# Fewer, wider loads of ready weight blocks, a summing transfer for one token group, and a late conversion with two load buffers

## The chip, the cores and the metric

The kernel runs on one core of a Trainium2 chip. The time is device microseconds of one execution, the median of several runs. The core's engines run side by side and each takes its instructions in order: TensorE (PE) multiplies, VectorE (DVE) and ScalarE (ACT) work element by element, GpSimd (POOL) does little arithmetic and issues transfers that add, and SyncE (SP) issues nearly all other transfers.

## The reference

Three layers follow one another: a masked attention over 2304 tokens with 8 heads of 64, a mixture of 8 experts whose weights per token come from eight normalizations by rows and columns, and a gated layer behind a row norm. All of it is wanted in float32.

```python
def _moe_ref(x, w_gate, w1, w2):
    ...
    for e in range(E):                       # E = 8, w1[e] 512 x 1024, w2[e] 1024 x 512
        h = np.maximum(x @ w1[e], 0.0)
        ye = h @ w2[e]
        out += P[:, e:e + 1] * ye
    return out

def _moe2_ref(x, w_gate, w_val, w_out, rms_g):   # w_gate, w_val 512 x 1536, w_out 1536 x 512
    rms = np.sqrt(np.mean(x * x, axis=-1, keepdims=True) + 1e-06)
    xn = x / rms * rms_g
    g = xn @ w_gate
    silu = g * (1.0 / (1.0 + np.exp(-g)))
    val = xn @ w_val
    return silu * val @ w_out
```

The last layer's three matrices, in_moe_w_gate, in_moe_w_val and in_moe_w_out in the profile, arrive as float64 and are turned into float32 on the chip.

## The kernel before, in words

**Split numbers.** A float32 product is made on PE from two rounded parts of each operand, a high one (made by ACT) and a low one (by DVE), with three matmuls. The 2304 tokens are three groups of 768 (qd 0, 1, 2), each of six tiles of 128 tokens.

**Fast products.** A block product of two by two blocks is done with seven products of sums of blocks instead of eight. The sums of x lie in DRAM, xdt for the experts and xnd for the last layer, and are loaded with 768-KB transfers (L1147). The sums of weights, "ready blocks", stand in w1t, for the last layer also in last_r, in slots of xt, and in w2t. Each of PE's products at L1215 is six matmuls of 128x384; the results go from PSUM through copies on ACT (L1383, L1401) and sums on DVE (L1247, L1404, L1418) in slots of a buffer fa: there are eight of these slots (zs), of 384 columns. The finished hidden values are split again (L1240, L1243) into ht and hx.

**The experts.** Expert 0 runs beside the attention, until about 480 us. Seven experts, two halves of the hidden width and three token groups make 42 groups of work, each of 14 products at L1215 and 14 units of nine matmuls at L1817. Units leave their sums in PSUM, and evict_1 takes them out to acc: an ACT copy (L1838) or a DVE addition (L1849), after which ACT multiplies by the token's weight (L1874) and POOL adds the piece by a transfer to y1d in DRAM (L1881). Only in the last expert's second half does DVE multiply and add straight from PSUM (L1843, 21 instructions for a token group); its first half has loaded y1d into acc by an adding transfer (L1883).

**The norm.** When a token group is complete, its rows are squared (ACT L1448), scaled (L1458), transposed by PE (L1465) and multiplied by rms_g (DVE L1466). norm_blocks then makes the seven sums and splits them (ACT L1482, DVE L1483, L1498 to L1504), and SP stores them in xnd (L1492 for the first three, L1516 for the others). For each tile the parts are built in the same few buffers (spare), so a tile's split waits until the store of the tile before has left them. This goes on during the next token group's units, and for the last group during the last layer's first products.

**The last layer.** Nine passes, three thirds of the hidden width by three token groups; each has 28 products at L1215 and 24 matmul groups into the output (L729 to L731), which DVE adds to acc (L2112) or ACT copies (L2110). The ready blocks of the first third are made during the experts by first_combos and kept in w1d in DRAM. ready_combos (L938) loads them: eight transfers earlier, and the other 32 in one row, behind the experts' last units.

**The conversion.** convert makes one half block of 128x256 numbers: load of the float64 halves to cv (L828, L831), seven DVE instructions (L836 to L860), store to m2g, m2v or m2o (L864). There are 72 of these items. 40 run in the expert stage and 32 from the second pass of the last layer on, in one load buffer; the stored tile t is also one buffer. m2o is loaded again (L1080) for w2t, where ACT (L1083) and DVE (L1086) split it.

**What sets the order.** A Background object counts slots, one for each product or unit. Queues of steps hang on it (fin, prep, prep2, conv); each step has a lag in slots behind the step before it. Everything is written in one order at build time, engines and the SP queue keep to it, and a wait holds up all that is behind on the same engine. At most eight transfers of SP are under way at once.

Of the kernel before, what the change touches and what calls it, by code (L numbers as in the profile page):

```python
# [8 lines left out]
F32 = mybir.dt.float32  # L9
F32R = mybir.dt.float32r  # L10
U32 = mybir.dt.uint32
# [103 lines left out]
def kernel(  # L115
# [48 lines left out]
    CONV_WAIT = (6, 4)  # L164
    PRE_WAIT = 6
    PRE_UNITS = 12
    LAG = 12
    TURN_AT = (29, 30, 31, 32, 33, 34), (32, 33, 34, 35, 36, 37)
# [650 lines left out]
    def convert(nm, f, half):  # L819

        n = KC * P // 2
        raw = cv[:, : 2 * n].bitcast(U32)
# [45 lines left out]
    def conversion(items, wait, quick=False):  # L868

        for n, (nm, f, half) in enumerate(items):  # L870
# [4 lines left out]
            step = 1 if quick else STEP  # L875
            conv.add([(wait, head), (step, number), (step, tail)], tag)
            if n + 1 < len(items):
                conv.add([(step, whole), (0 if quick else 1, convert(*items[n + 1])[0])], tag)
                conv.add([(0 if quick else 2, store)], tag)
            else:  # L880
                conv.add([(step, whole), (WRITE, store)], tag)


    SPOTS = (0, 1, 5, 2, 3, 4, 6)

    def first_combos(s, c):
# [35 lines left out]
        def store(src, n0, n):  # L922
            for i, t in enumerate((h[:, : src.shape[1]], src)):
                nc.sync.dma_start(out=w1d[:, s, i, n0 : n0 + n, c], in_=t.rearrange("p (k n) -> p k n", k=n))
# [3 lines left out]
            (1, lambda: store(raw, 0, 4)), (5, lambda: high(both)), (STEP, lambda: low(both)),  # L928
            (1, lambda: store(both, 4, 3)),
        ]  # L930

    def ready_combos(g, j, part):

        at = region(g, j)
        for k, n in ((), ((0, 2),), ((3, 2),), ((5, 1), (6, 1)), ((2, 1),))[part]:
            p = SPOTS.index(k)
            for i in range(2):
                nc.sync.dma_start(  # L938
                    out=at(7 * i + k, n).bitcast(F32).rearrange("p (k m) -> p k m", k=n),
                    in_=w1d[:, j, i, p : p + n].rearrange("p k c m -> p k (c m)"),  # L940
                )
# [111 lines left out]
    def prepare_1(g, j, part=None):  # L1053
# [5 lines left out]
        if g == E:  # L1059
            prep.add([(PACE, lambda: ready_combos(g, j, part))], ("w1", g, j))  # L1060
# [159 lines left out]

    def h_slot(i):
        t = ht_flat[:, 768 * i : 768 * (i + 1)] if i < 4 else hx[:, i - 4]
        return t[:, :TH], t[:, TH:]
# [301 lines left out]
    with tc.manual_schedule():  # L1525
# [300 lines left out]
        def evict_1(n, k):  # L1826
# [36 lines left out]
            if (g, hh) == (E - 1, 1) and k >= 5:  # L1863
                scales[k - 5].add(norm_scale(qd, 3 * (k - 5)), ("scale", qd))
# [364 lines left out]
```

## Time and profile before

| | us |
|---|---|
| median of 3 runs | 2128.11 (2127.64 to 2130.58) |
| profiled execution | 2127.49, of which its span 2124.7 |
| PE busy | 2027.7, 95% of the span |
| DVE busy | 1594.4, 75% |
| ACT busy | 1312.5, 62% |
| POOL busy | 268.4, 13% |
| mean granted clock of PE | 0.985 of full speed |

A profile is of one execution. Attention with expert 0 fills the time to about 480 us, the other experts that to about 1632, the last layer the rest. The changeover from experts to last layer lies between 1570 and 1735 us. An idle stretch of an engine is given in square brackets with what ended it; where several things were waited for, the one that came last by the profile is named.

### The profile page before, as it was taken

To read this page: it belongs to the slowest core of one execution; us is meant where nothing else is said; L and a number is where in the kernel's file an instruction comes from. 1 tells how busy PE (TensorE), PEld (TensorE's weight loads), DVE (VectorE), ACT (ScalarE), POOL (GpSimd) and SP (SyncE) were. 2 spreads that over 40 slices of the span, in tenths; PEclk is the share of its full clock that TensorE was granted. 3 is DMA by queue.
4 is the path that set the end of the run, shared out by engine and by line. 5 is a ranking of instruction groups with operands and counts; after the bars stand their busy time and mean duration, and the time that the engine had idled before them with its cause. 6 is when DMAs were issued, how large, how long until landed. Compare 5 with 4: busy or idle time off the path is not lost. (4 is left out here: it accounts for less than half of the span.)

```text
span 2124.7 us, 37479 instructions
## 1 busy us (share of the span) xinstructions
PE 2027.7 (95%) x13611; PEld 1926.7 (91%) x13611; DVE 1594.4 (75%) x3387; ACT 1312.5 (62%) x2932; POOL 268.4 (13%) x304
## 2 busy tenths in 40 slices
PE   8999998999999999999999999999997689999998
PEld 7888888999999999999999999999997578888897
DVE  4677656878787887868778787887987567877644
ACT  6766334777776877778777777777755333423422
POOL 6444200001111111111111111111100000000000
PEclk9999999999999999999999999999998899999999
DMA  7687675577978979798887978869657764443331
GB/s 188 165 247 197 197 250 181 210 247 178 279 210 216 264 204 296 202 245 224 237 250 193 264 185 239 225 165 281 185 158 261 232 202 155 131 174 115 129 134 60
DMA packets 358249, 434.24 MB, mean 204 GB/s; under 512 B 80944, under 2 KB 260336, under 8 KB 358064
## 3 DMA queue, kind: packets, MB, share of 16 engines
q1 hardware_dynamic: 319296, 363.48, 52.2%
q0 software_dynamic: 38768, 68.36, 18.6%
q8 instruction: 107, 1.75, 0.3%
q14 instruction: 78, 0.64, 0.1%
HBM read 301.75 MB, written 130.02 MB: 203 GB/s over the span
## 5 line engine op out<-in xcount | busy, mean ns | idle before, releaser
L1215 PE MATMUL ub<-xt,w1t 128*128 128x384 f32 x2328 | 475.4, 341 | 29.2 <-DVE fa L1404 14.2
L1215 PEld LDWEIGHTS ub<-xt,w1t 128*128 128x128 f32 x2328 | 401.5, 192 | 36.5 <-DVE fa L1404 14.8
L1215 PE MATMUL ub<-xx,w1t 128*128 128x384 f32 x1956 | 396.4, 339 | 10.5 <-DVE fa L1247 3.8
L1817 PE MATMUL db<-w2t,ht 128*128 128x256 f32 x2772 | 383.0, 283 | 6.5 <-DVE acc L1849 3.3
L1817 PEld LDWEIGHTS db<-w2t,ht 128*128 128x128 f32 x2772 | 368.2, 190 | 11.1 <-DVE acc L1849 7.1
L1817 PE MATMUL db<-w2t,hx 128*128 128x256 f32 x2520 | 349.6, 284 | 7.2 <-DVE acc L1849 3.8
L1215 PEld LDWEIGHTS ub<-xx,w1t 128*128 128x128 f32 x1956 | 333.8, 190 | 18.4 <-DVE fa L1247 6.9
L1817 PEld LDWEIGHTS db<-w2t,hx 128*128 128x128 f32 x2520 | 333.2, 190 | 16.2 <-DVE acc L1849 12.5
L1247 DVE TENSOR_TENSOR fa<-ub,fa 128x384 f32<-128x384 f32 x360 | 199.2, 554 | 149.2 <-PE ub L1215 134.9
L1366 ACT ACTIVATE fa<-fa 128x384 f32<-128x384 f32 x252 | 132.3, 525 | 180.6 <-DVE fa L1247 180.3
L1881 POOL DMA_DIRECT2D y1d<-acc x99 | 113.9, 1150 | 843.6 <-ACT acc L1874 378.3
L1243 DVE TENSOR_TENSOR ht<-fa,ht 128x384 fp32r<-128x384 f32 x344 | 189.4, 552 | 33.0 <-ACT ht L1240 32.3
L1240 ACT ACTIVATE ht<-fa 128x384 fp32r<-128x384 f32 x344 | 177.4, 518 | 37.9 <-DVE fa L1418 37.4
L1874 ACT ACTIVATE acc<-acc,prob 128x256 f32<-128x256 f32 (+1 forms) x351 | 190.8, 573 | 14.3 <-DVE acc L1849 14.0
L1243 DVE TENSOR_TENSOR hx<-fa,hx 128x384 fp32r<-128x384 f32 x316 | 174.4, 552 | 27.9 <-ACT hx L1240 26.6
L1240 ACT ACTIVATE hx<-fa 128x384 fp32r<-128x384 f32 x316 | 162.1, 519 | 48.7 <-DVE fa L1418 47.4
L1321 DVE TENSOR_TENSOR fa<-fa 128x384 f32<-128x384 f32 x336 | 185.6, 552 | 5.3 <-ACT fa L1362 0.3
L1358 ACT COPY fa<-ub 128x384 f32<-128x384 f32 x252 | 119.7, 475 | 94.9 <-PE ub L1215 90.8
L1849 DVE TENSOR_TENSOR acc<-db,acc 128x768 f32<-128x768 f32 (+1 forms) x117 | 143.0, 1222 | 33.3 <-PE db L1817 32.1
L1838 ACT COPY acc<-db 128x768 f32<-128x768 f32 x156 | 124.5, 798 | 19.8 <-PE db L1817 16.8
L1383 ACT COPY fa<-ub 128x384 f32<-128x384 f32 x108 | 51.4, 477 | 92.0 <-PE ub L1215 91.8
L981 DVE TENSOR_TENSOR w1t<-fa,w1t 128x256 fp32r<-128x256 f32 (+1 forms) x160 | 83.4, 525 | 11.1 <-ACT w1t L978 10.7
(261 smaller groups left out, 3070.2 us busy)
## 6 DMA issues: line engine op xcount, KB each, us to landing
xt<-xdt SPq DMA_DIRECT2D x111, 768.0 KB
xx<-xdt SPq DMA_DIRECT2D x92, 768.0 KB
y1d<-acc POOLq DMA_DIRECT2D x72, 384.0 KB, 7.0
y1d<-acc POOLq DMA_DIRECT2D x36, 768.0 KB, 8.1
xt<-xnd SPq DMA_DIRECT2D x25, 768.0 KB
xx<-xnd SPq DMA_DIRECT2D x24, 768.0 KB
fa<-in_moe_w_dram SPq DMA_DIRECT2D x56, 256.0 KB
raw<-in_moe_w_dram SPq DMA_DIRECT2D x52, 256.0 KB
```

Source lines behind the costliest of these rows:

```text
L1215: nc.tensor.matmul(ps[:, :TH], w[i][:, c], x[:, k, c], start=first and c == 0 and n == 0, stop=c == 1 and n == 2, skip_group_check=True,)
L1240: nc.scalar.activation(h[0], src, func)
L1243: engine.tensor_tensor(out=h[1], in0=src, in1=h[0].bitcast(F32), op=ALU.subtract)
L1247: nc.vector.tensor_tensor(out=out, in0=ps, in1=more, op=ALU.add)
L1321: nc.vector.tensor_tensor(**kw)
L1358: nc.scalar.copy(z[nm], ps)
L1366: nc.scalar.activation(z[nm], z[nm], AF.Relu)
L1817: nc.tensor.matmul(spot(k, m), hm[x], w[y], start=BEGIN[k] and r == 0 and m in FIRST[PAIR[k]] and i == 0, stop=r == 1 and i == 2, skip_gro ...
L1838: nc.scalar.copy(a, ps)
L1849: nc.vector.tensor_tensor(out=a, in0=ps, in1=a, op=ALU.add)
L1874: nc.scalar.activation(a, a, AF.Copy, scale=prob[:, tile_of(qd, b), g : g + 1])
L1881: nc.gpsimd.dma_start(out=y, in_=t, accum_op=ALU.add)
```

## The change

The edits, in the order of the diff:

- The ready blocks lie in w1d in the order in which they are used, so that they come back with 14 transfers instead of 40; each of the eight stores of first_combos becomes ten transfers instead of four. The last two column blocks come back as they lie, in pieces of up to 128x3072 (L2094 of the new file).
- The late conversion (late_conversion) uses a second load buffer, which is two neighbouring slots of the eight in fa, from the second pass to the end. A load is issued two items ahead. The conversion rests in every third pass. Eight items of w_out more are done in the expert stage, 48 instead of 40, with a pause of 4 slots instead of 6 before each; the late ones have 3.5 instead of 4.
- Of the last expert, the middle token group (qd 1) goes the way of the other experts: its first half adds to y1d, its second half is copied or added to acc, weighted by ACT, and y1d is added to acc by three transfers of POOL. Its norm starts 14 and 16 slots later (GATHER), and its tiles are transposed three slots later, the sixth of them in the last layer's first pass.

New line numbers are higher by 10 to 21 in the places below: L938 is L949 and L2094, L1080 L1090, L1083 L1093, L1147 L1157, L1448 L1466, L1458 L1476, L1482 L1500, L1492 L1510, L1516 L1534, L1240 L1258, L828 and L831 L829 and L832, L864 L865.

```diff
     EARLY_AT = (5, 6)
     SUMS = 24
-    CONV_WAIT = (6, 4)
-    PRE_WAIT = 6
+    CONV_WAIT = (4, 3.5)
+    PRE_WAIT = 4
+    GATHER = 14, 16
     PRE_UNITS = 12
     LAG = 12
-    TURN_AT = (29, 30, 31, 32, 33, 34), (32, 33, 34, 35, 36, 37)
+    TURN_AT = (29, 30, 31, 32, 33, 34), (35, 36, 37, 38, 39)
     BLOCK_LAG = (1.0, 1.0, 0.85)
...
-    def convert(nm, f, half):
+    def convert(nm, f, half, raw=None):
 
         n = KC * P // 2
-        raw = cv[:, : 2 * n].bitcast(U32)
+        raw = (cv[:, : 2 * n] if raw is None else raw).bitcast(U32)
...
-    def conversion(items, wait, quick=False):
+    def late_conversion(items, wait, other):
+
+        made = [convert(*x, (None, other)[n % 2]) for n, x in enumerate(items)]
+        conv.add([(WRITE, made[0][0]), (0, made[1][0])], items[0][:2])
+        for n, (_, head, number, tail, whole, store) in enumerate(made):
+            tag = items[n][:2]
+            conv.add([(wait, head), (1, number), (1, tail), (1, whole)], tag)
+            if n + 2 < len(made):
+                conv.add([(0, made[n + 2][0])], tag)
+            conv.add([(0, store)], tag)
...
-        def store(src, n0, n):
-            for i, t in enumerate((h[:, : src.shape[1]], src)):
-                nc.sync.dma_start(out=w1d[:, s, i, n0 : n0 + n, c], in_=t.rearrange("p (k n) -> p k n", k=n))
+        def store(src, spots):
+            for i, t in enumerate((h, src)):
+                for at, k, n in spots:
+                    nc.sync.dma_start(
+                        out=w1d[:, s, i, k : k + n, c],
+                        in_=t[:, P * at : P * (at + n)].rearrange("p (k n) -> p k n", k=n),
+                    )
 
         return load, [
             (PRE_WAIT, sums_1), (STEP, sums_2), (STEP, lambda: high(raw)), (STEP, lambda: low(raw)),
-            (1, lambda: store(raw, 0, 4)), (5, lambda: high(both)), (STEP, lambda: low(both)),
-            (1, lambda: store(both, 4, 3)),
+            (1, lambda: store(raw, ((0, 0, 2), (2, 5, 1), (3, 2, 1)))), (5, lambda: high(both)), (STEP, lambda: low(both)),
+            (1, lambda: store(both, ((0, 3, 2), (2, 6, 1)))),
...
-    def ready_combos(g, j, part):
-
-        at = region(g, j)
-        for k, n in ((), ((0, 2),), ((3, 2),), ((5, 1), (6, 1)), ((2, 1),))[part]:
-            p = SPOTS.index(k)
-            for i in range(2):
-                nc.sync.dma_start(
-                    out=at(7 * i + k, n).bitcast(F32).rearrange("p (k m) -> p k m", k=n),
-                    in_=w1d[:, j, i, p : p + n].rearrange("p k c m -> p k (c m)"),
-                )
+    def ready_combos(j, part):
+
+        k, n = ((0, 0), (0, 2), (3, 2), (5, 2), (2, 1))[part]
+        if n:
+            to = w1_flat[:, 3584 * j : 3584 * (j + 1)].rearrange("p (i k m) -> p i k m", i=2, k=7)
+            nc.sync.dma_start(
+                out=to[:, :, k : k + n].bitcast(F32), in_=w1d[:, j, :, k : k + n].rearrange("p i k c m -> p i k (c m)")
+            )
...
+        def pair(self):
+            n = next(n for n in range(7) if all(any(x is y for x in self.free) for y in z_all[n : n + 2]))
+            self.free = [x for x in self.free if not any(x is y for y in z_all[n : n + 2])]
+            return fa[:, 1536 + TH * n : 1536 + TH * n + 512]
...
+    zs = Store(z_all)
...
+            direct = (g, hh) == (E - 1, 1) and qd != 1
+            if not direct and k in (0, 2, 3, 4):
                 bg.drain(("expert", qd, half, col if half else None))
                 nc.scalar.copy(a, ps)
-            elif (g, hh) == (E - 1, 1):
+            elif direct:
...
+                if not direct:
+                    scales[k - 5].follow([(GATHER[k - 5], lambda: None)], ("scale", qd))
                 scales[k - 5].add(norm_scale(qd, 3 * (k - 5)), ("scale", qd))
...
-                elif g < E - 1:
+                elif g < E - 1 or (hh, qd) == (0, 1):
...
-        conv_items += [(nm, f, half) for f in range(NG, 2 * NG) for nm in "gv" for half in range(2)]
-        conv_items += [("o", f, half) for f in range(NG, 2 * NG) for half in range(2)]
+        conv_items += [(nm, f, half) for f in range(NG, 2 * NG) for nm in "gvo" for half in range(2)]
...
-                conversion(conv_items[24:40], CONV_WAIT[0])
+                conversion(conv_items[24:48], CONV_WAIT[0])
...
-        for j in (2, 3):
-            for part in range(1, 5):
-                ready_combos(E, j, part)
+        for j, parts in (
+            (2, ((last_r[:, :1792], 0), (x_slot(gone_x)[:, :1280], 7), (last_r[:, 1792:], 12), (x_slot(gone_x)[:, 1280:], 13))),
+            (3, ((w2t[:, 0:3].rearrange("p f s n -> p (f s n)"), 0), (xt_flat[:, 7680:8192], 12))),
+        ):
+            ready = w1d[:, j].rearrange("p i k c m -> p (i k c m)")
+            for t, at in parts:
+                nc.sync.dma_start(out=t.bitcast(F32), in_=ready[:, 256 * at : 256 * at + t.shape[1]])
...
+            conv.paused = n % NQD == NQD - 1
             if n == 1:
                 conv.yields = False
-                conversion(conv_items[40:], CONV_WAIT[1], True)
+                late_conversion(conv_items[48:], CONV_WAIT[1], zs.pair())
...
+                            if step == 0:
+                                turn_tile(1, 5, db[5], spares[NGP - 2])
```

**Order of instructions, place 1.** SP, between the x loads of the first pass and the norm stores of the last group (w1t, last_r, xt, w2t hold ready blocks; xnd<-acc and xnd<-cv are those stores). Before, from the m2o loads on:

```order
L1080 DMA fa<-m2o 128x512
L1492 DMA xnd<-acc 128x6x128 x2
L1080 DMA fa<-m2o 128x512
L938 DMA w1t<-w1d 128x256 x6
L938 DMA w1t<-w1d 128x512 x4
L938 DMA w1t<-w1d 128x256 x6
L938 DMA last_r<-w1d 128x512
...
L938 DMA xt<-w1d 128x256
L938 DMA w2t<-w1d 128x256 x2
L1516 DMA xnd<-acc 128x4x128 x2
L1516 DMA xnd<-acc 128x2x128
```

Now:

```order
L1090 DMA fa<-m2o 128x512 x2
L949 DMA w1t<-w1d 128x2x256
L949 DMA w1t<-w1d 128x2x512 x3
L949 DMA w1t<-w1d 128x2x256
L2094 DMA last_r<-w1d 128x1792
L2094 DMA xt<-w1d 128x1280
L2094 DMA last_r<-w1d 128x256
L2094 DMA xt<-w1d 128x256
L2094 DMA w2t<-w1d 128x3072
L2094 DMA xt<-w1d 128x512
L1510 DMA xnd<-acc 128x6x128 x2
L1534 DMA xnd<-acc 128x4x128 x2
```

Eleven wide loads stand where 32 stood. The pair of L1492 stores, which stood between the two m2o loads, now comes behind the loads.

**Place 2.** ACT, at the end of the experts (w2t<-fa is the split of a loaded m2o, acc<-acc,cv the scaling of a tile's rows, cv<-acc the squares). Before:

```order
L1458 ACTIVATE acc<-acc,cv 128x512 x2
L1240 ACTIVATE ht<-fa 128x384
L1458 ACTIVATE acc<-acc,cv 128x512
L1240 ACTIVATE hx<-fa 128x384 x2
L1240 ACTIVATE ht<-fa 128x384
L1482 ACTIVATE acc<-acc 128x512
L1482 ACTIVATE acc<-acc 128x256
L1083 ACTIVATE w2t<-fa 128x512
L1448 ACTIVATE cv<-acc 128x512
L1482 ACTIVATE acc<-acc 128x256
```

Now:

```order
L1476 ACTIVATE acc<-acc,cv 128x512
L1466 ACTIVATE xt,cv<-acc 128x512
L1476 ACTIVATE acc<-acc,cv 128x512
L1093 ACTIVATE w2t<-fa 128x512
L1466 ACTIVATE cv<-acc 128x512
L1476 ACTIVATE acc<-acc,cv 128x512
L1466 ACTIVATE cv<-acc 128x512
L1476 ACTIVATE acc<-acc,cv 128x512 x2
L1466 ACTIVATE cv<-acc 128x512
L1500 ACTIVATE acc<-acc 128x512
L1500 ACTIVATE acc<-acc 128x256
```

The scalings of a group's last tiles stood ahead of the m2o split; now three of them stand behind it.

**Place 3.** SP, in the second pass of the last layer (cv and fa<-in_moe_w are loads of conversion items, m2o, m2g, m2v<-cv their stores, xx and xt<-xnd the x loads of the next pass). Before:

```order
L828 DMA cv<-in_moe_w_out_dram 128x512
L864 DMA m2o<-cv 128x256
L1147 DMA xx<-xnd 128x2x768 x2
L1147 DMA xt<-xnd 128x2x768
L828 DMA cv<-in_moe_w_out_dram 128x512
L864 DMA m2o<-cv 128x256
L1147 DMA xt<-xnd 128x2x768 x3
L828 DMA cv<-in_moe_w_out_dram 128x512
```

Now:

```order
L832 DMA fa<-in_moe_w_val_dram 128x2x256
L865 DMA m2g<-cv 128x256
L832 DMA cv<-in_moe_w_val_dram 128x2x256
L865 DMA m2v<-cv 128x256
L1157 DMA xx<-xnd 128x2x768
L832 DMA fa<-in_moe_w_val_dram 128x2x256
L865 DMA m2v<-cv 128x256
L1157 DMA xx<-xnd 128x2x768
L1157 DMA xt<-xnd 128x2x768 x2
L832 DMA cv<-in_moe_w_gate_dram 128x2x256
```

Loads alternate between cv and fa, and each stands ahead of the store of an item; the stores still come from cv alone.

## Rows read from the trace of the kernel before

**Rows 1.** The page's part 1: engine, busy us (share of the span), instructions.

```profile
PE 2027.7 (95%) x13611; PEld 1926.7 (91%) x13611; DVE 1594.4 (75%) x3387; ACT 1312.5 (62%) x2932; POOL 268.4 (13%) x304
```

**Rows 2.** 480 to 1560: width, PE, PEld, DVE, ACT, POOL, clock, DMA share, GB/s.

```profile
480.00:1560.00 1080.00, 1069.76 (x7503) 1056.23 (x7502) 882.90 (x1766) 813.18 (x1694) 136.75 (x123) 1.00 0.84 226
```

**Rows 3.** Waits of PE, whole span: us in total, times, longest us.

```profile
PE ub L1215 <- DVE fa L1404: 18.2, 6, 14.0
```

**Rows 4.** Timeline of PE: start us, us, instruction, count [idle before <-releaser].

```profile
1602.07 2.29 PE L1817 MATMUL db<-w2t,hx 128*128 128x256 f32 x9 [3.34 <-DVE acc L1843]
...
1660.66 2.29 PE L1215 MATMUL ub<-xt,w1t 128*128 128x384 f32 x6 [13.96 <-DVE fa L1404]
1662.75 1.05 PE L1465 MATMUL db<-ident,acc 128*128 128x128 f32 x4
```

**Rows 5.** Timeline of ACT, changeover.

```profile
1632.29 0.63 ACT L1083 ACTIVATE w2t<-fa 128x512 fp32r<-128x512 f32 x1 [6.06 <-PE ub L1215]
...
1658.80 0.42 ACT L1482 ACTIVATE acc<-acc 128x256 fp32r<-128x256 f32 x1 [12.85 <-DMA xnd<-acc]
```

**Rows 6.** Timeline of SP, changeover: DMA issues.

```profile
1614.86 0.87 SPq L1147 DMA_DIRECT2D xt<-xnd  x2
...
1634.06 8.24 SPq L938 DMA_DIRECT2D w1t<-w1d  x16
...
1654.90 1.73 SPq L1516 DMA_DIRECT2D xnd<-acc  x3
```

**Rows 7.** Last layer in pieces, one pass long (columns as in rows 2).

```profile
1731.49:1782.40 50.91, 48.11 (x240) 43.89 (x240) 35.59 (x90) 17.53 (x36) 0.00 (x0) 0.97 0.52 178
1782.40:1830.73 48.33, 47.26 (x240) 42.53 (x240) 43.70 (x111) 22.71 (x49) 0.00 (x0) 1.00 0.30 94
1830.73:1886.52 55.79, 48.83 (x241) 42.10 (x241) 44.35 (x110) 18.61 (x39) 0.00 (x0) 1.00 0.53 182
1886.52:1939.20 52.68, 48.84 (x240) 44.00 (x241) 41.49 (x100) 15.52 (x33) 0.00 (x0) 0.97 0.46 162
1939.20:1987.25 48.05, 46.23 (x241) 42.71 (x241) 31.44 (x62) 18.59 (x40) 0.00 (x0) 1.00 0.16 52
...
2034.69:2082.11 47.42, 46.21 (x240) 42.68 (x240) 23.13 (x42) 13.78 (x28) 0.00 (x0) 1.00 0.41 150
```

**Rows 8.** Waits of DVE, 1700 to 2125.

```profile
DVE cv L836 <- DMA cv<-in_moe_w_out_dram: 11.9, 9, 2.7
...
DVE cv L836 <- DMA cv<-in_moe_w_val_dram: 5.9, 3, 3.7
...
DVE cv L837 <- DMA m2o<-cv: 1.1, 5, 0.3
```

**Rows 9.** Lines of DVE, 1570 to 1612: shapes, count | busy us, mean ns.

```profile
L1843 DVE SCALAR_TENSOR_TENSOR acc<-db,prob,acc 128x256 f32<-128x256 f32 x18 | 7.6, 477 | 1.5 <-PE db L1817 1.5
...
L1843 DVE SCALAR_TENSOR_TENSOR acc<-db,prob,acc 128x512 f32<-128x512 f32 x3 | 2.1, 743 | 0.0
```

**Rows 10.** Lines of DVE, 480 to 1560.

```profile
L1849 DVE TENSOR_TENSOR acc<-db,acc 128x768 f32<-128x768 f32 x70 | 66.8, 955 | 0.7
```

**Rows 11.** 10-us pieces of the changeover (columns as in rows 2).

```profile
1620.00:1630.00 10.00, 9.55 (x76) 9.22 (x75) 8.67 (x18) 0.42 (x1) 0.00 (x0) 0.94 1.03 404
...
1650.00:1660.00 10.00, 0.00 (x0) 0.00 (x0) 0.76 (x2) 1.20 (x4) 0.00 (x0) 0.60 0.95 302
```

**Rows 12.** Timeline of SP: that item's load, and the store before it.

```profile
1862.26 0.37 SPq L831 DMA_DIRECT2D cv<-in_moe_w_val_dram  x1
...
1863.52 0.33 SPq L864 DMA_DIRECT2D m2v<-cv  x1
```

**Rows 13.** Timeline of DVE: one item's first and second instruction.

```profile
1869.59 0.29 DVE L836 TENSOR_SCALAR cv<-cv 128x256 uint32<-128x256 uint32 x1 [3.70 <-DMA cv<-in_moe_w_val_dram]
...
1870.04 0.29 DVE L837 TENSOR_SCALAR cv<-cv 128x256 f32<-128x256 f32 x1 [0.15 <-DMA m2v<-cv]
```

**Rows 14.** Lines of DVE, 1731 to 1987: one of an item's seven instructions.

```profile
L854 DVE SCALAR_TENSOR_TENSOR cv<-cv 128x256 f32<-128x256 uint32 x30 | 12.8, 426 | 1.0
```

More of the change, by code (lines that the diff above doesn't have):

```diff
@@ L866, in convert, with conversion @@
         return load, head, number, tail, whole, store
-    def conversion(items, wait, quick=False):
+    def late_conversion(items, wait, other):
[7 more added lines that the diff above has]
+            conv.add([(0, store)], tag)
+    def conversion(items, wait):
         for n, (nm, f, half) in enumerate(items):
@@ L874, in conversion @@
                 conv.add([(WRITE, load)], tag)
-            step = 1 if quick else STEP
-            conv.add([(wait, head), (step, number), (step, tail)], tag)
+            conv.add([(wait, head), (STEP, number), (STEP, tail)], tag)
             if n + 1 < len(items):
-                conv.add([(step, whole), (0 if quick else 1, convert(*items[n + 1])[0])], tag)
-                conv.add([(0 if quick else 2, store)], tag)
-            else:
-                conv.add([(step, whole), (WRITE, store)], tag)
-    SPOTS = (0, 1, 5, 2, 3, 4, 6)
+                conv.add([(STEP, whole), (1, convert(*items[n + 1])[0]), (2, store)], tag)
+            else:
+                conv.add([(STEP, whole), (WRITE, store)], tag)
     def first_combos(s, c):
@@ L1059, in prepare_1 @@
         if g == E:
-            prep.add([(PACE, lambda: ready_combos(g, j, part))], ("w1", g, j))
+            prep.add([(PACE, lambda: ready_combos(j, part))], ("w1", g, j))
         else:
@@ L1219, in product, with h_all @@
         bg.matmuls(6, TH)
+    def h_all(i):
+        return ht_flat[:, 768 * i : 768 * (i + 1)] if i < 4 else hx[:, i - 4]
     def h_slot(i):
-        t = ht_flat[:, 768 * i : 768 * (i + 1)] if i < 4 else hx[:, i - 4]
-        return t[:, :TH], t[:, TH:]
+        return h_all(i)[:, :TH], h_all(i)[:, TH:]
     class Store:
@@ L1234, in give @@
             self.free.append(x)
-    zs = Store(fa[:, 1536 + TH * n : 1536 + TH * (n + 1)] for n in range(8))
+        def pair(self):
+            n = next(n for n in range(7) if all(any(x is y for x in self.free) for y in z_all[n : n + 2]))
+            self.free = [x for x in self.free if not any(x is y for y in z_all[n : n + 2])]
+            return fa[:, 1536 + TH * n : 1536 + TH * n + 512]
+    z_all = [fa[:, 1536 + TH * n : 1536 + TH * (n + 1)] for n in range(8)]
+    zs = Store(z_all)
     hslots = Store(range(8))
@@ L1835, in evict_1 @@
                 a = a[:, :, 256 * col : 256 * (col + 1)]
-            if (hh == 0 or g < E - 1) and k in (0, 2, 3, 4):
+            direct = (g, hh) == (E - 1, 1) and qd != 1
+            if not direct and k in (0, 2, 3, 4):
                 bg.drain(("expert", qd, half, col if half else None))
                 nc.scalar.copy(a, ps)
-            elif (g, hh) == (E - 1, 1):
+            elif direct:
                 if k in (0, 2, 3):
@@ L1856, in evict_1 @@
                     prepare_2(E, (0, 2, 1, 3)[k - 3])
-            if (hh == 0 or g < E - 1) and k in (1, 5, 6):
+            if not direct and k in (1, 5, 6):
                 args = (g, hh, qd) + ((1, 0) if k == 1 else (0, None) if k == 5 else (1, 1))
```

## The prediction, made before the changed kernel ran

> **What bounds the kernel now.** I read the page's first part, then PE's waits of the stretch between the experts and the last layer, then the timelines of the engines named there, then equal pieces of the last layer. TensorE (PE) is busy 95% of the span [rows 1], so only the places where it stands still, or runs at the lower of its two clock levels, are to be had. In the expert stage there is next to nothing: from 480 to 1560 us it stands still for 10.2 of 1080 us while VectorE (DVE) is 82% busy [rows 2]. Two places remain.
>
> The first is the changeover. PE waits 18.2 us in six places for one line of VectorE, 14.0 of it at a single product [rows 3]; the row transposes behind that product start only at 1662.75 [rows 4]. The reader should go back along the chain: PE waits for DVE, DVE for ScalarE (ACT), and ACT waits 12.85 us, from 1645.95 to 1658.80, for the store xnd<-acc, whose source it is to overwrite [rows 5]. SP issues that store only at 1654.90, after 32 loads of ready blocks that began at 1634.06 [rows 6]. These follow a load of m2o that stood behind seven 768-KB loads of x from 1614.86 on, and the ACT conversion that needs it starts at 1632.29 [rows 5, 6]. So it is one transfer queue, not arithmetic.
>
> The second is the late conversion. Seven pieces of the last layer, each a pass long, run from one late eviction to the next. The ones without conversion take 47.42 us; the four with most of it take 50.91, 48.33, 55.79 and 52.68 [rows 7]: 18.0 us too many, with 0.6 in the fifth, 18.7 in all. VectorE waits there for loads of raw halves 11.9 and 5.9 us [rows 8].
>
> **Part by part: A, the changeover.** Call the time when the m2o load lands T; it was 1632.3. Three things move.
>
> (1) The middle token group's evictions. Before, 21 VectorE instructions, 7.6 + 2.1 = 9.7 us [rows 9]. After, four go to ACT as copies, and three stay on VectorE as one instruction each, two of 0.955 us [rows 10] and one of twice the width, about 1.8 (an estimate by width): 3.7 us. VectorE is relieved by 6 us between 1577 and 1605, and PE's 3.34 us wait at 1602.07 for such an eviction [rows 4] goes. The stores of x that release the seven loads depend on that stretch, so the loads can start earlier: 2 us if only part of the relief arrives, 5 if also the lower clock after it goes (the nine matmuls there take 2.29 us). I take 3.5. The 17.4 us from 1614.86 to 1632.3 are bytes (5.5 MB at about 0.33 MB/us) and stay. T is then about 1629.
>
> (2) The ACT conversion of m2o now stands ahead of the last three row scalings (second pair of order listings), so PE's transposes wait for T as well. This costs PE nothing of its own: what stands behind has until the stores land. But it leaves PE idle before T and makes it do two units and eight products after T.
>
> (3) The ready loads. 5.77 MB in 11 loads instead of 6.29 MB in 32, and the first two xnd stores (0.39 MB each) of the last group now stand behind all of them (first pair of listings), as the wide store of 1654.90 did before. Each load waits only for free blocks, so they begin about T+2. What does the queue move? 302 GB/s in 1650 to 1660 with its engines 95% busy, on pieces of 1 and 2 KB; 404 GB/s in 1620 to 1630 on the x loads' 3-KB pieces [rows 11]. Of the new loads 3.67 MB come in whole rows of up to 12 KB, so I price them at 404 (9.1 us), the other 2.1 MB and the second m2o load at 302 (7.8 us), and the two stores at 302 (2.6 us): the stores land at T+21.5. Then an ACT copy, three VectorE steps and a transpose follow, 2.5 us: PE goes on at T+24 = 1653, where it stood at 1662.75 before [rows 4]. A = -10 us. Bounds: everything at 302 GB/s and T only 2 us earlier gives 1630.3 + 2 + 22.6 + 2.5 = 1657.4, so -5; all at 404 and T 5 earlier gives 1627.3 + 2 + 16.9 + 2.5 = 1648.7, so -14.
>
> The Trainium skill, DMA: Bandwidth & Descriptors, section "Anatomy of one DMA", fits a transfer as 2.0 us plus bytes at 436 GB/s. By an estimate from that page the 5.77 MB would take 15.2 us, and A would be about -12; no row here shows 436 GB/s, the best is 404.
>
> **B, the rest of the changeover.** The same transposes, splits and stores follow as before, shifted; their waits stay. They now meet the x loads of the next pass a little sooner: between 0 and +3, taken +1.
>
> **C, the late conversion.** Eight of 32 items leave, and pass 2 (of nine, from 0) and pass 5 rest. From the order of instructions, items begin in passes 1 to 5 as 7, 7, 8, 7, 3 before and 8, 0, 8, 8, 0 after. The items that leave are those of the two cheap passes: 48.33 - 47.42 = 0.9 us [rows 7], and 0.6. The dear passes, 1, 3 and 4, are those with x loads; two of them get one item more. At 3.49/7 and 5.26/7 us each that is +1.2. Net -0.3.
>
> The second load buffer is the question. Before, SP issues the next load and right behind it the store of the item just made, at 1862.26 and 1863.52 [rows 12]. The next item's first instruction waits 3.70 us for the load; its second, which overwrites the stored tile, waits a further 0.15 for the store [rows 13]. So the store lands within half a microsecond of the load. Over the last layer the second instruction waits only 1.1 us for m2o stores [rows 8], because the first has already waited. The tile that is stored has no second buffer after the change, and the third pair of listings shows the store still behind a load. Prefetching takes away the wait that is named and leaves the one beneath it. I take 0.3 us of gain for each of some ten waits, against heads that come half a slot sooner and wait that much longer: 0 together. C = 0, with +4 if the heads' half slot is paid in full, and -9 if half of the 18.7 us goes.
>
> **D, two of eight product slots.** The second buffer takes two of the eight slots that hold a product on its way from PSUM, through all later passes. In the order of instructions 30 instead of 15 of 108 ACT copies then wait for a VectorE reader, 19 of them one that is only two to four instructions back. The nearest price is what PE lost at that reader before, outside the changeover: 18.2 - 14.0 = 4.2 us in five places [rows 3]. Twice as many such waits may cost as much again; with PE's lead as it is they may cost nothing. Between 0 and +4, taken +1.5.
>
> **E, the expert stage.** Eight items of seven VectorE instructions (289 to 426 ns, the longest in [rows 14]; together 2.43 us) are 19.5 us more, on an engine with 197 us to spare [rows 2]. They run with pauses of 4 slots instead of 6, and end at the same product as before. Nothing, or half as much again as PE's 10.2 us of standing still there, 5 us; taken +1. The 48 more stores on SP, 64 KB each or less, ride in the time before the next x loads: 0.
>
> **Sum.** -10 + 1 + 0 + 1.5 + 1 = -6.5, against the profiled execution's 2127.5: 2121.0. The median of the runs is 0.6 us above that execution: **2121.5 us**.
>
> **The rivals.** R1, prefetch pays: the store needs no longer than the work between two items, and only the load's wait was real. Half of the excess goes, C = -9, 2112.5 us. For it: the load is the wait that is named, 17.8 us of it. Against: the store's 0.15 us right behind. The Trainium skill, DMA: Bandwidth & Descriptors, section "Rules for kernel authors", advises issuing a transfer early and waiting late; followed here, it gives this rival's time, and the row on the store speaks against it.
>
> R2, the changeover only moves: the loads go on at 302 GB/s, T comes 2 us sooner, later waits return 2 more. A + B = -5 + 3, with D and E 2128.0. For it: the stores still stand behind nearly as many bytes.
>
> R3, slower: six slots are too few. Its place is the ACT copy of each product in passes 1 to 8. If a pass loses 2 us there (16 rounds at 1 us), D is +16: 2136. It decides from about 1.5 us a pass. The piece from 1782.40 on, with VectorE 90% busy (43.70 of 48.33 us), lost only 0.9 [rows 7], which speaks against it; for it speaks that slots were never this few.
>
> R4, the whole block runs at 404 GB/s and PE keeps its higher clock: A = -14, B = 0, 2116.5 us.
>
> **Chances.** Forecast 0.43, R1 0.20, R2 0.20, R3 0.10, R4 0.07. A measurement of this kernel tells about 0.2%, 4.3 us, from no change: faster means below 2123.9. R1, R4 and four fifths of the forecast lie there, 0.62; R2 and the rest of the forecast are the same, 0.28; R3 is slower, 0.10. The range leaves out R3 and the lower end of R1: 2110 to 2131.
>
> **What would show it.** Changeover: m2o landing near 1629, one PE gap before it and one ending at 1650 to 1657 whose chain leads to xnd<-acc, and no 32-fold block on SP. Conversion: VectorE's waits at the first instruction of an item nearly gone, and waits for m2 stores at the second of about the same sum; pieces with conversion still 3 to 8 us over 47.4. If those waits vanish too, C was wrong and R1 holds. Slots: pieces without conversion at 47.4 to 47.9; above 48.5 R3 is at work. Experts: PE idle from 480 to 1560 us below 15 us. The forecast fails if T does not come earlier, or if the store is not what ends last.

## The result and the profile after

The changed kernel takes 2156.5 us (median of 4 runs, 2153.5 to 2159.9) where the kernel before takes 2128.8: ratio 1.013, 95% interval 1.011 to 1.015. It is 28 us slower, where 2121.5 with 2110 to 2131 was forecast. The profiled execution took 2156.46 us, its span 2154.7.

PE's work is the same, 2029.9 us instead of 2027.7 [rows 1]; PE waits more. To find where, I compared the times of one and the same instruction in both traces. The evictions' ACT copies (L1838, now L1857) are good marks, since they come in the same order in both. The 141st of them, shortly before the expert stage ends:

```profile
1416.88 0.80 ACT L1838 COPY acc<-db 128x768 f32<-128x768 f32 x1
```

in the kernel before, and in the changed one

```profile
1445.19 0.80 ACT L1857 COPY acc<-db 128x768 f32<-128x768 f32 x1 [0.18 <-PE db L1835]
```

So 28.3 us were lost by then. The 21st copy stands at 508.19 and 506.44; the **expert piece** between the two marks takes 908.7 us before and 938.8 after. From the 141st copy to the first late eviction (1731.49 and 1759.74), the **changeover piece**, it is 314.6 and 314.6; from there to the last late eviction (2082.11 and 2111.26), the **last-layer piece**, 350.6 and 351.5. All of the loss lies in the expert stage, the stage that was priced at +1. The row that answers to [rows 2] shows it: in the same 1080 us, PE stands still for 33.9 us instead of 10.2 and gets 228 fewer matmuls done, while DVE is busy less, not more.

```profile
480.00:1560.00 1080.00, 1046.08 (x7275) 1029.12 (x7275) 867.94 (x1766) 794.55 (x1654) 134.59 (x121) 0.99 0.83 222
```

DVE's waits for transfers in the expert stage, 480 to 1560 (us in total, times, longest), add up to 69.8 us:

```profile
DVE cv L909 <- DMA cv<-m2v: 16.3, 2, 8.6
...
DVE cv L838 <- DMA m2g<-cv: 16.1, 6, 4.1
...
DVE cv L838 <- DMA m2o<-cv: 11.8, 4, 4.1
...
DVE cv L837 <- DMA cv<-in_moe_w_val_dram: 9.4, 2, 5.0
DVE cv L837 <- DMA cv<-in_moe_w_out_dram: 8.5, 2, 5.2
...
DVE cv L838 <- DMA m2v<-cv: 3.4, 2, 1.9
DVE cv L837 <- DMA cv<-in_moe_w_gate_dram: 3.2, 1, 3.2
...
DVE cv L909 <- DMA cv<-m2g: 1.1, 1, 1.1
```

In the kernel before they were 21.6 us:

```profile
DVE cv L837 <- DMA m2g<-cv: 7.2, 3, 3.2
...
DVE cv L901 <- DMA cv<-m2g: 4.9, 1, 4.9
DVE cv L901 <- DMA cv<-m2v: 2.8, 1, 2.8
...
DVE cv L836 <- DMA cv<-in_moe_w_val_dram: 2.5, 1, 2.5
DVE cv L836 <- DMA cv<-in_moe_w_out_dram: 1.9, 1, 1.9
...
DVE cv L837 <- DMA m2v<-cv: 1.1, 2, 0.7
DVE cv L836 <- DMA cv<-in_moe_w_gate_dram: 0.9, 1, 0.9
...
DVE cv L837 <- DMA m2o<-cv: 0.3, 1, 0.3
```

L909 is the first instruction of a block sum (first_combos), L837 and L838 the first two of an item. The largest stall shows how it comes about. SP, in the changed kernel:

```profile
936.49 1.14 SPq L1157 DMA_DIRECT2D xt<-xdt  x2
937.68 1.29 SPq L903 DMA_DIRECT2D cv<-m2v  x2
```

Then DVE, and behind it PE:

```profile
943.01 0.42 DVE L994 TENSOR_TENSOR fa<-fa 128x256 f32<-128x256 f32 x1
952.02 0.62 DVE L909 TENSOR_TENSOR cv<-cv 128x128 f32<-128x128 f32 x2 [8.59 <-DMA cv<-m2v]
```

```profile
954.10 2.29 PE L1225 MATMUL ub<-xx,w1t 128*128 128x384 f32 x6 [6.52 <-DVE fa L1265]
```

The two loads of the block sum, 128 KB each, were issued at 937.7 behind two 768-KB loads of x, and their reader could start 14 us later. DVE came to that reader after 5.8 us, stood there for 8.59, and all that PE waited for stood behind it; PE then ran its next six matmuls at the lower clock (granted 0.50 from 952 to 954), 2.29 us instead of the 1.21 of the six before the stall. Over these 14 us (columns as in [rows 2]) the transfer engines were full:

```profile
938.00:952.00 14.00, 9.58 (x69) 9.38 (x68) 3.41 (x7) 5.06 (x11) 1.86 (x2) 0.91 1.06 274
```

The pause of 6 slots had been the cover for such a load, and the change cut it to 4. The Trainium skill, DMA: Bandwidth & Descriptors, section "Queues, rings and completion order", says that each DMA engine takes the descriptors of a queue's ring in their order; these rows agree as far as they go, 14 us for 256 KB issued behind x loads on the same queue. But order is not all of it: 14 us at 274 GB/s are some 3.8 MB, more than the 1.5 MB just ahead. Three more x loads had been issued since 929.9, and two adding transfers of POOL, on another queue, took 11.1 and 10.4 us in the same stretch. How much each of them cost, no run separates.

Only a quarter of the 69.8 us (17.4) is at block sums. At items, 21.1 us are for loads and 31.3, the most, at L838 for the store of the item before, which frees the one tile t: the pause covered both.

In the changeover (timeline of ACT, then of SP and of PE):

```profile
1661.70 0.63 ACT L1093 ACTIVATE w2t<-fa 128x512 fp32r<-128x512 f32 x1 [13.99 <-DMA fa<-m2o]
...
1684.35 0.94 ACT L1500 ACTIVATE acc<-acc 128x512 fp32r<-128x512 f32 x2 [3.77 <-DMA xnd<-acc]
```

```profile
1644.85 0.87 SPq L1157 DMA_DIRECT2D xt<-xnd  x2
...
1663.46 2.48 SPq L949 DMA_DIRECT2D w1t<-w1d  x5
```

```profile
1663.61 1.12 PE L1483 MATMUL db<-ident,acc 128*128 128x128 f32 x4 [13.42 <-ACT acc L1476]
...
1687.31 1.08 PE L1483 MATMUL db<-ident,acc 128*128 128x128 f32 x4 [5.31 <-DVE acc L1484]
```

From the 141st copy on, the x loads start after 199.7 us (before 198.0), the m2o load is used after 216.5 (before 215.4), the store that ACT waits for has landed 22.7 us after that (before 26.5, from [rows 5]), and PE's transposes go on after 242.1 (before 245.9). These 3.8 us are given back in the next 70 us.

The last layer's pieces (columns as in [rows 2]), which answer to [rows 7]:

```profile
1759.74:1809.02 49.28, 46.50 (x240) 42.65 (x241) 30.02 (x72) 17.51 (x36) 0.00 (x0) 1.00 0.46 159
1809.02:1855.93 46.91, 46.24 (x240) 42.64 (x240) 34.29 (x79) 22.94 (x49) 0.00 (x0) 1.00 0.20 60
1855.93:1914.55 58.62, 51.02 (x240) 45.19 (x240) 46.43 (x115) 18.59 (x39) 0.00 (x0) 0.94 0.54 180
1914.55:1967.99 53.44, 49.43 (x241) 45.34 (x241) 37.07 (x85) 15.63 (x33) 0.00 (x0) 0.94 0.42 140
```

and DVE's waits in them, from 1725 on:

```profile
DVE cv L838 <- DMA m2v<-cv: 9.8, 6, 2.9
...
DVE cv L838 <- DMA m2o<-cv: 6.3, 5, 2.7
...
DVE cv L838 <- DMA m2g<-cv: 3.6, 4, 1.2
DVE cv L837 <- DMA cv<-in_moe_w_gate_dram: 1.1, 1, 1.1
```

An item as in [rows 13], now:

```profile
1887.57 0.29 DVE L837 TENSOR_SCALAR cv<-fa 128x256 uint32<-128x256 uint32 x1
...
1890.80 0.29 DVE L838 TENSOR_SCALAR cv<-cv 128x256 f32<-128x256 f32 x1 [2.95 <-DMA m2v<-cv]
```

The load is there, and the store is waited for at the next instruction.

### The profile page after: what moved, and what is told of

It is laid out like the page before. It is cut to its first block, busy times and chain, and to the rows that moved or that the text cites. A ratio compares the mean times of both kernels' runs of the same rounds, so it can differ in the third digit from the quotient of the medians.

```text
span 2154.7 us, 37548 instructions
## 1 busy us (share of the span) xinstructions
PE 2029.9 (94%) x13611; PEld 1928.0 (89%) x13611; DVE 1586.3 (74%) x3369; ACT 1319.0 (61%) x2945; POOL 271.1 (13%) x307
## 4 chain that ended last, share of the span: by engine, by line
PE 60%; DVE 16%; DMA 15%; ACT 4%; issue 2%; SPq 1%; POOL 1%; DVEq 0%; POOLq 0%; ACTq 0%
PE ub L1225 27%; PE db L1835 19%; DMA m2o<-cv 3%; DMA m2g<-cv 3%; DMA m2v<-cv 2%; DVE fa L1265 2%; DVE acc L1868 2%; PE db L730 2%; PE db L731 2%; PE db L732 2%; DVE ht L1261 1%; DVE hx L1261 1%; DMA cv<-m2v 1%; PE psh L730 1%; DMA xnd<-acc 1%
## 5 line engine op out<-in xcount | busy, mean ns | idle before, releaser
L1265 DVE TENSOR_TENSOR fa<-ub,fa 128x384 f32<-128x384 f32 x360 | 199.7, 555 | 145.4 <-PE ub L1225 131.3
L1895 ACT ACTIVATE acc<-acc,prob 128x256 f32<-128x256 f32 (+1 forms) x360 | 195.9, 573 | 18.0 <-DVE acc L1868 17.8
L1258 ACT ACTIVATE ht<-fa 128x384 fp32r<-128x384 f32 x344 | 177.5, 518 | 45.1 <-DVE fa L1436 43.1
L1258 ACT ACTIVATE hx<-fa 128x384 fp32r<-128x384 f32 x316 | 162.5, 519 | 47.2 <-DVE fa L1436 45.7
L1857 ACT COPY acc<-db 128x768 f32<-128x768 f32 x160 | 127.8, 799 | 18.9 <-PE db L1835 16.1
```

Of the source, the lines that this page charges most:

```text
L1258: nc.scalar.activation(h[0], src, func)
L1265: nc.vector.tensor_tensor(out=out, in0=ps, in1=more, op=ALU.add)
L1857: nc.scalar.copy(a, ps)
L1895: nc.scalar.activation(a, a, AF.Copy, scale=prob[:, tile_of(qd, b), g : g + 1])
```

## Experiments

The three pieces, taken between the marks above in each run's trace, in us. Where two programs share a piece, its values show the spread: the expert piece of the four runs with pauses of 6 and four stores (before, e6, e7, e8) lies between 907.9 and 919.0. The ratios are each to the kernel before as it ran beside that run.

| kernel | median (runs) | ratio to before, 95% | expert piece | changeover piece | last-layer piece |
|---|---|---|---|---|---|
| before | 2128.8 | | 908.7 | 314.6 | 350.6 |
| changed | 2156.5 (4) | 1.011 to 1.015 | 938.8 | 314.6 | 351.5 |
| e1 pauses and items back | 2154.4 (2) | 1.007 to 1.018 | 912.9 | 315.4 | 372.6 |
| e2 before, short pauses | 2155.8 (2) | 1.009 to 1.017 | 935.7 | 313.8 | 354.1 |
| e3 pause 6 for sums | 2145.1 (4) | 1.005 to 1.011 | 920.0 | 321.0 | 352.3 |
| e4 four stores | 2155.4 (2) | 1.009 to 1.016 | 941.3 | 312.5 | 349.8 |
| e5 wide alone | 2125.1 (10) | 0.996 to 1.000 | 906.1 | 310.8 | 354.4 |
| e6 sum alone | 2130.3 (10) | 0.999 to 1.003 | 909.0 | 316.5 | 353.6 |
| e7 load buffers alone | 2133.5 (10) | 1.000 to 1.004 | 919.0 | 315.4 | 356.0 |
| e8 load and store buffers | 2114.8 (4) | 0.989 to 0.995 | 907.9 | 315.9 | 338.1 |
| e9 wide and both buffers | 2112.5 (6) | 0.989 to 0.995 | 916.0 | 310.3 | 336.6 |
| e10 and the sum | 2117.0 (10) | 0.993 to 0.997 | 918.0 | 316.4 | 336.6 |
| e11 changed, store buffer | 2139.7 (9) | 1.003 to 1.007 | 940.7 | 313.1 | 336.5 |
| e12 pause 8 for sums | 2107.7 (6) | 0.988 to 0.992 | 909.3 | 310.8 | 336.6 |

### The expert stage: e1 to e4

**e1**, the changed kernel:

```diff
-    CONV_WAIT = (4, 3.5)
-    PRE_WAIT = 4
+    CONV_WAIT = (6, 3.5)
+    PRE_WAIT = 6
...
-                conversion(conv_items[24:48], CONV_WAIT[0])
+                conversion(conv_items[24:40], CONV_WAIT[0])
```

with the late conversion from item 40 on; the items stay in the changed kernel's order, w_out among the others.

> The changed kernel with its expert-stage conversion as before: pauses of 6 slots ahead of items and of block sums, 40 items there and 32 late; wide loads, ten stores a block sum, two load buffers and the summing transfer stay. The changed kernel lost about 30 us between 480 and 1540 us and came out level from there to the end of the experts. Theory P (the pauses were the cover for a load or a store that stands in SP's queue behind x and weight loads; 4 slots are too short): the expert stage is back within 4 us of the kernel before, time 2126 to 2131. Rival S (the ten smaller stores per block sum hold up SP and the transfer engines): the stage stays some 25 us long, time 2148 to 2155.

The expert piece is back at 912.9, 4.2 us above the kernel before and within the spread, as theory P has it; rival S is out. The time, 2154.4 where 2126 to 2131 was expected, is not back, and that I had overlooked: 32 late items do not fit in passes 1, 3 and 4, and the last eight begin from 1976 to 2024, where the weights that they make are already wanted; PE stands still for 8.26 us at 1986.3. The last-layer piece is 21 us longer than the changed kernel's.

**e2**, the kernel before:

```diff
-    CONV_WAIT = (6, 4)
-    PRE_WAIT = 6
+    CONV_WAIT = (4, 4)
+    PRE_WAIT = 4
```

> The kernel before with nothing changed but the expert-stage pauses, 6 to 4 slots for items and for block sums; 40 items and four stores a block sum stay. Theory P: the expert stage gets 20 to 30 us longer, in steps where VectorE waits for a load or store of the conversion; time 2148 to 2158, and items end earlier in the program. Rival S, or rival N (the eight more items are what VectorE can't carry): 2127 to 2133.

27.0 us longer in the expert piece, 2155.8 us in all, with nothing else changed. DVE's waits, 480 to 1560, the two largest (in this kernel L901 is the block sum's first instruction and L837 an item's second):

```profile
DVE cv L901 <- DMA cv<-m2v: 16.4, 3, 8.5
DVE cv L837 <- DMA m2g<-cv: 13.2, 5, 4.5
```

This is the loss, from the pauses alone. It needs neither the eight items (rival N) nor the ten stores.

**e3**, the changed kernel with `PRE_WAIT = 6`.

> The changed kernel with only the pause ahead of block sums back at 6 slots; items keep 4. The two largest stalls of the changed kernel in the experts, 6.5 and 5.7 us of TensorE, follow waits of 8.6 and 7.8 us for loads that block sums read. Theory P: these two go, some 12 to 15 us with what the lower clock cost, the other half of the loss stays; time 2140 to 2146. Rival S: no change, 2153 to 2158. Three slots' worth of items end later than in the changed kernel, at the end of the experts' conversion.

2145.1 us, 11 less. The expert piece is 11.3 over the kernel before instead of 30.1, so the sums' pause is worth some 19 us. The other 11 go with the items' pause: DVE's waits at items are still 44.4 us, where the kernel before has 13.9. Their price is less sure, since 920.0 is only just above the 919.0 of a run with pauses of 6. The changeover piece gives 6 us of the gain back: at 1529.15, after the 141st copy, PE stands still for 7.47 us while DVE, which had waited 4.85 us for an item's load, does the rest of that item at one go. What is left at block sums:

```profile
DVE cv L909 <- DMA cv<-m2v: 3.5, 1, 3.5
```

**e4**, the changed kernel, first_combos:

```diff
-            (1, lambda: store(raw, ((0, 0, 2), (2, 5, 1), (3, 2, 1)))), (5, lambda: high(both)), (STEP, lambda: low(both)),
-            (1, lambda: store(both, ((0, 3, 2), (2, 6, 1)))),
+            (1, lambda: store(raw, ((0, 0, 4),))), (5, lambda: high(both)), (STEP, lambda: low(both)),
+            (1, lambda: store(both, ((0, 4, 3),))),
```

> The changed kernel with four stores for each block sum instead of ten, in the order in which the blocks lie in SBUF, so that the ready blocks come back in other places than the products want them (the last layer's first third is wrong, its work the same). Theory P: nothing, or up to 5 us less, since SP's own issue time is not what VectorE waits for: 2150 to 2157. Rival S: most of the 30 us goes, 2126 to 2132.

No gain, 2155.4 us and an expert piece of 941.3. The 48 more stores on SP cost nothing that can be seen.

### The changeover: e5 and e6

**e5** is the kernel before with the edits of store, ready_combos and the bulk loads (L2094 of the changed kernel), **e6** the kernel before with those of `direct`, GATHER, TURN_AT and the gather's condition.

> The kernel before with only the new layout of the ready blocks: ten stores a block sum, 14 wide loads instead of 40. Theory W (the prediction's third step: what ends last is the store behind the loads, and wide loads move more in a microsecond): the store that ACT waits for lands 3 to 5 us sooner after the m2o load than the 26.5 us of before, TensorE goes on that much sooner, and part is given back behind it; 2123 to 2127. Rival (later waits in the changeover take all of it): 2127 to 2131.

The m2o split and the split that waits for the store, on ACT in e5:

```profile
1632.95 0.63 ACT L1084 ACTIVATE w2t<-fa 128x512 fp32r<-128x512 f32 x1 [6.98 <-DMA fa<-m2o]
...
1656.44 0.42 ACT L1491 ACTIVATE acc<-acc 128x256 fp32r<-128x256 f32 x1 [10.05 <-DMA xnd<-acc]
```

23.5 us after the m2o load instead of 26.5, and the changeover piece 3.8 us shorter: theory W. The other runs bear it out: without the summing transfer, the piece is 310.3 to 310.8 in the three runs with wide loads (e5, e9, e12) and 313.8 to 315.9 in the four without. The 3.0 us of the medians (2125.1 against 2128.1 on that chip) are at the edge of what can be measured. e5's last-layer piece, 3.8 us above the kernel before's, is no return of the gain: e2 and e6, without the wide loads, have 354.1 and 353.6.

> The kernel before with only the middle token group's summing transfer and its later norm. The prediction's first step: VectorE is relieved and the x loads, and with them the m2o load, start about 3.5 us sooner; 2123 to 2127. Theory G, from the changed kernel, where they started 1.8 us later: the relief reaches TensorE before the x loads but not their stores, and TensorE then stands idle for the m2o load in front of the row scalings, so that work is left for after it; x loads no sooner than before, time 2127 to 2135.

```profile
1613.95 0.87 SPq L1148 DMA_DIRECT2D xt<-xnd  x2
```

```profile
1630.73 0.63 ACT L1084 ACTIVATE w2t<-fa 128x512 fp32r<-128x512 f32 x1 [12.71 <-DMA fa<-m2o]
```

From the 141st copy of this run (1413.72) the x loads start after 200.2 us and the m2o load is used after 217.0: 2.3 and 1.6 later than before, not 3.5 earlier. ACT now stands 12.71 us in front of the m2o split with the scalings behind it. Theory G holds in that the x loads come no sooner. The piece, 316.5, is 1.9 us longer than in the kernel before, 0.6 above the longest of the runs that share its loads. Beside the wide loads the price is clearer: 312.5 to 316.4 with the summing transfer in the changed kernel, e1, e4, e10 and e11 (and 321.0 in e3, with its stall at 1529), 310.3 to 310.8 without it. Why the x loads start later, I did not settle: the stores that release them are issued 1 us later and land about 1 us later, with three more transfers of POOL under way, but no run separates these.

### The late conversion: e7, e8 and e11

**e7** is the kernel before with late_conversion, Store.pair and 3.5 slots, without rests. **e8** adds

```diff
-        a, t = cv[:, 2 * n : 3 * n].bitcast(U32), cv[:, 3 * n : 4 * n]
+        a, t = cv[:, 2 * n : 3 * n].bitcast(U32), cv[:, 3 * n : 4 * n] if made is None else made
...
-        made = [convert(*x, (None, other)[n % 2]) for n, x in enumerate(items)]
+        made = [convert(*x, (None, other[:, :512])[n % 2], (None, other[:, 512:])[n % 2]) for n, x in enumerate(items)]
```

where `other` is now all 768 columns of the two product slots; 256 of them had been left unused.

> The kernel before with only the late conversion's two load buffers and its pause of 3.5 slots; 32 late items, no rest in any pass, two of the eight product slots taken. Theory L (the store of the item before lands last): waits at an item's first instruction nearly gone, waits at its second 15 to 25 us in all, time unchanged or a little longer, 2127 to 2134. Rival R1 of the prediction (only the load's wait was real): 2117 to 2122.

> The run before it with a second buffer for the stored tile too, in what is left of the two product slots. Theory L: now both waits go, to less than 6 us together, and the time is 4 to 9 us below the run with load buffers alone, 2119 to 2127. Rival D (the conversion's pace and the lost slots, not its waits, make the passes long): waits go but the time stays at that of the run with load buffers alone.

In e7 DVE's waits from 1700 on have moved from the loads to the stores, as theory L has it: 26.1 us at the second instruction, just over the 25 expected. Together they are 29.2, where the kernel before has 20.5 (19.0 for loads, 1.5 for stores):

```profile
DVE cv L838 <- DMA m2o<-cv: 14.1, 12, 3.0
...
DVE cv L838 <- DMA m2v<-cv: 7.8, 6, 2.8
...
DVE cv L838 <- DMA m2g<-cv: 4.2, 4, 1.6
...
DVE cv L837 <- DMA cv<-in_moe_w_out_dram: 3.1, 1, 3.1
```

e7 is 5 us longer in the last layer, not shorter. e8 is 17.9 us shorter there than e7 and 12.5 shorter than before; in all, by the medians, 13 us faster than the kernel before, more than the 2119 to 2127 that was expected. Its pieces:

```profile
1728.95:1775.86 46.91, 46.23 (x240) 42.70 (x241) 37.46 (x94) 17.59 (x36) 0.00 (x0) 1.00 0.57 196
1775.86:1824.33 48.47, 47.12 (x241) 42.37 (x241) 44.86 (x115) 22.71 (x49) 0.00 (x0) 1.00 0.32 96
1824.33:1874.77 50.44, 47.04 (x240) 42.50 (x240) 45.92 (x113) 18.54 (x39) 0.00 (x0) 1.00 0.59 200
1874.77:1922.26 47.49, 46.28 (x240) 42.67 (x240) 37.48 (x86) 15.63 (x33) 0.00 (x0) 1.00 0.50 171
```

and all of DVE's waits for conversion transfers from 1700 on:

```profile
DVE cv L837 <- DMA cv<-in_moe_w_out_dram: 3.2, 1, 3.2
```

In these four pieces the excess over 47.42 is 3.6 us instead of the 18.0 of before, with as many items, the same pace and the same six product slots as in e7. So the waits made the passes long (rival D is out), and the six slots cost next to nothing. The rule of the Trainium skill that the prediction set against the row on the store (DMA: Bandwidth & Descriptors, "Rules for kernel authors": issue early, wait late) holds once both transfers have it.

> The changed kernel with nothing but a second buffer for the stored tile of the late conversion. Theory L: the 19.7 us of waits at the second instruction of an item go, passes 1, 3 and 4 get 2, 8 and 4 us shorter, time 2141 to 2148, all of it in the last layer; the expert stage keeps its loss of 25 to 30 us. Rival D: 2153 to 2158.

The same edit in the changed kernel: the last-layer piece gets 15 us shorter, and the expert piece stays 32 us above the kernel before's. The time, 2139.7, lies just below the expected range.

### Putting the good parts together: e9, e10 and e12

**e9** is e8 with the wide loads, **e10** e9 with the summing transfer, **e12** e9 with `PRE_WAIT = 8`.

> The kernel before with the wide ready loads and with two load and two store buffers for the late conversion; expert-stage pauses of 6, 40 items there, no rest, no summing transfer. Theories W and L add up, since the one acts in the changeover and the other in passes 1 to 4: 13 us from the buffers and 3 from the loads, ratio 0.990 to 0.995, 2108 to 2117. Rival (what the changeover gains comes back in the later passes, as half of it did in the run with wide loads alone): no faster than the buffers alone, ratio 0.992 or above.

> The run before it and the summing transfer with its later norm. Theory G: the first wait for m2o stands ahead of the row scalings and TensorE does after it what it could have done before; 1 to 4 us slower than without. The prediction's first step: 3 us faster than without.

> The run with wide loads and both buffers (e9), with the pause ahead of block sums 8 slots instead of 6. In that run, with 6, one wait of 8.5 us for a block sum's load stood in the expert stage, where the kernel before had 4.9, and the stage was 7 us longer than before, in a part of the program that the run had not changed but for its stores. Theory P, taken the other way: the waits at block sums fall below 4 us in all, the expert stage is at or below the 908.7 us of before, time 2103 to 2110. Rival: 6 slots were enough, and the difference is chance; 2110 to 2115.

e9's changeover and last-layer pieces are 4.3 and 14.0 us shorter than before, so the gains add up there. The times do not show it: e9 has 2112.5 us and a ratio of 0.992, e8 on another chip 2114.8 and 0.992, so that the rival is out by the pieces alone. e9's profiled execution lost 7.3 us of the gain in an expert stage that shares its pauses with the kernel before, where DVE waits

```profile
DVE cv L909 <- DMA cv<-m2g: 8.5, 1, 8.5
DVE cv L838 <- DMA m2g<-cv: 8.2, 3, 4.5
...
DVE cv L837 <- DMA cv<-in_moe_w_gate_dram: 3.6, 1, 3.6
```

Behind the 8.5 PE stands still for 5.24 us at 951.4; behind an item that waits 3.62 for its load and then 4.46 for the store before it, for 4.75 us at 674.3. Three of the eight runs with pauses of 6 (e7, e9, e10) have the wait of 8.5 us, the other five 4.6 to 5.2 at the same place. e10's median is 4.5 us above e9's, with intervals that overlap; its changeover piece is 6.1 longer, as with the summing transfer elsewhere: theory G.

e12 takes 2107.7 us, ratio 0.990 (0.988 to 0.992), the fastest of all and faster than both kernels, 22 us below the kernel before on its chip. At the place of the 8.5 us DVE waits 0.7; at block sums it still waits 5.9 us in all, more than the 4 I expected, and 909.3 is not below 908.7. The stall at 674 is gone as well, which the sums' pause does not explain. Between e12 and e9 the intervals just overlap (0.988 to 0.992 and 0.989 to 0.995), so that the longer pause pays is likely and not proven.

## Why the prediction was wrong

The forecast of -6.5 us missed mainly by one term: E is 29 us off. A and B, forecast at -9 together and measured at 0, are another 9.

- **E, the expert stage, failed**: +1 forecast with a bound of +5, +30 measured. The step that failed is "They run with pauses of 4 slots instead of 6". It priced DVE's work (19.5 us against 197 us to spare) and the end of the items, and took the shorter pause for harmless. A pause in front of an instruction that reads a load, or that overwrites what a store still reads, is what hides that transfer: with 4 slots DVE waited 69.8 us for them, and PE stood still for 33.9 us where below 15 had been given as the sign. The rows of before had the warning: even with 6 slots DVE waited 21.6 us for these transfers. e2 shows the loss from the pauses alone (27.0 us), e3 that 19 of the changed kernel's 30 us went with the sums' pause, e4 and e2 clear the stores and the items. The same trap had been seen in part C, where the half slot got a bound of +4; the two slots of the expert stage were not asked the same question.
- **A, the changeover**: -10 forecast, -3.8 where PE's transposes go on. Step 3 was right in kind and nearly in size: the store landed 22.7 us after the m2o load (21.5 forecast), PE went on 25.6 us after it (24), and the queue moved 403 and 415 GB/s from 1670 to 1675 and 1675 to 1680, near the 404 of the price. The fit that the prediction cites beside it (the Trainium skill, "Anatomy of one DMA") is given there for GpSimd's transfers, and these are SP's; the forecast did not use it. Step 1 failed: PE's 3.34 us wait, which was to go, only fell to 2.76, and the x loads started 1.7 us later, not 3.5 earlier, so that the m2o load was used 1.1 later; e6 shows it alone. The step took for granted that the stores of x follow DVE's pace. That T does not come earlier had been named as a sign that the forecast fails.
- **B**: +1 forecast, +3.8. The later waits took back all of A in the changed kernel; not in e5 and e9, where the scalings stand ahead of the m2o split. R2, with A and B at -2 together, came nearest here, though not by the 302 GB/s that it rests on. (Its 2128.0 lacks the 0.6 us from the profiled execution to the median that the other sums have.)
- **C, the late conversion, was right** in mechanism and in its sum: waits for loads 1.1 us, waits for stores 19.7, the excess over 47.42 in the five pieces 19.5 us (1.9 - 0.5 + 11.2 + 6.0 + 1.0) where 18.7 + 1.5 had been forecast with D. Piece by piece it was less right: the three with most of the conversion are 1.9, 11.2 and 6.0 over, not 3 to 8 each, so that the sum came out as well as it did partly by luck. e7 and e8 show the reason.
- **D**: +1.5 forecast, next to nothing measured. The last three pieces, 48.38, 47.45 and 47.44 us in the changed kernel, were 48.05, 47.44 and 47.43 before. In e8 they are 48.38, 48.97 and 47.43; the 48.97 goes with a granted clock of 0.97, and e6, with all eight slots, has 48.96 there. Rival R3 is out.
- Of the rivals, R1 (prefetch pays) gives e8's time only when the store is freed too. The slower side was expected from the product slots; it came from the pauses, which no rival named.

## What to carry to other kernels

A pause that a schedule puts ahead of an instruction is a price paid for some transfer: before shortening it, read in the trace how long the load or store behind it takes to land at its worst, with the large transfers that can stand ahead of it in the queue, and what else stands behind the waiting instruction. The wait that the profile names is the one that ended last; ask which one ended just before it, since a second buffer for the first wait alone gains nothing (e7), and one for both gains 13 us (e8). Price a change in every stage that it touches by its waits, not by the engine's spare time.

## What was not expected of the hardware

A load of 256 KB was there after 2.8 us in the last layer (issued 1738.82, read 1741.64 in the kernel before), with the transfer engines 0.43 busy; two loads of 128 KB took 14 us behind x loads and beside POOL's adding transfers, with the engines full. Executions of programs that agree in the expert stage differ there by up to 11 us (907.9 to 919.0), with one wait of 8.5 us where others have 5.2 or less, so that a difference of a few us in one execution says little; the pieces and the medians of several runs say more.
